# Laying out a collecting tile by branch in a convolution-stem backward kernel

## The chip, the core and the metric

The kernel runs on one core of one Trainium2 chip. The metric is device time in microseconds (us), from the first to the last instruction of one execution; a kernel's time is the median of several executions. The core has four compute engines that work side by side: TensorE (PE) multiplies, VectorE (DVE) and ScalarE (ACT) work element by element and empty the accumulators (PSUM) of PE, GpSimd (POOL) fills and issues transfers. SyncE (SP) computes nothing; its queue issues most DMA transfers. Each engine runs its own list of instructions strictly in order, and an instruction starts when the semaphores that it names have reached their values.

## The reference

The forward pass is a one-dimensional convolution (31 taps, stride 2, 256 channels in and out, 2 sequences of 16000 rows), then a normalisation over time per channel, then GELU. The kernel returns the forward output and the gradients of the input `x`, the weights and the normalisation's scale and shift:

```python
h = jnp.einsum('blc,cd->bld', x[:, 0:s * L:s, :], w[0])
for i in range(1, K):
    h = h + jnp.einsum('blc,cd->bld', x[:, i:i + s * L:s, :], w[i])
...
_out, _vjp = jax.vjp(_f, x, w, gn_gamma, gn_beta)
_grads = _vjp(grad_out)
```

Nearly everything is bfloat16; products are accumulated in float32.

## The kernel before, in words

One big tile named `arena` (211104 bytes on each of the 128 partitions) holds nearly all working data. The function `sb(offset, shape)` cuts views out of it by byte offset, and different stages reuse the same bytes. In the profile, therefore, almost every operand is called `arena`, and work is told apart by its line.

The program is planned first and emitted afterwards. A `Plan` collects all operations; a table of 3528 numbers, `SEQUENCE`, then gives the one order in which they are emitted. So each engine's list is fixed by that table. The semaphore waits are not written in the kernel: the framework adds them when an operation touches bytes of a tile that an earlier operation of another engine or of a DMA reads or writes.

The stages are: forward (matmuls at line 564), input gradient (matmuls at line 1244, stages G0 and G1), weight gradient (line 1522). The change lies in the first part of the input gradient, G0, which runs from about 410 to 605 us and covers three quarters of sequence 0. Interleaved with it, DVE and ACT still work off the GELU backward of sequence 1 (function `gelu_unit`: L922 and L920, L925, L927 and L929, L931, five L935, L946 and L948). The last L935 of each unit needs a piece of `grad_out` that arrives transposed by DMA (L355). Its result is written to a buffer in memory by a DMA of SP (`dyd`).

G0 has six rounds, numbered here 0 to 5: three chunks `c`, two halves `pr` each. The convolution is computed in the manner of a fast (Toom-like) product, with three branches in the order B, A, C, and each branch has leaves A and C beside a shared middle leaf. For branch B the two results are kept in float32 in the tile `GRB` (ACT, L659). For branches A and C, a result that PE has left in PSUM is added to `GRB` by one DVE instruction, L1347, and written to the tile `HO` as bfloat16. A round thus has four such evacuations, written here branch/leaf: A/A, A/C, C/A, C/C; 24 in the six rounds. After both leaves of a branch are there, one SP transfer of 512 KB stores that branch's half rows to `out_1` (L1350 in the source, recorded as L350, the line of the helper `load`). There is one `HO` for all rounds.

The table `SEQUENCE` mixes the rounds' steps. In round 4 the order is A/A, C/A, A/C, store A, C/C, and the store of C comes after A/A of round 5. In round 5 it is A/A, store C of round 4, A/C, C/A, store A, C/C; the store of C comes much later.

Steps that the prediction names: the seed of a branch (`g_seed`, ACT L659 from PSUM to PSUM) copies PSUM banks after the middle leaf and can only write banks that DVE has emptied; the middle leaf's own copy is ACT L1277; `first`, `second`, `third` (L1142, L1192) are DVE differences that make PE's operands; L513 are DVE sums of weights; `dl_turn` transposes planes by SP (L355) and stores them by POOL (`dld`). In the round after the sixth (stage G1) the tile `HO` is replaced by two tiles `HOS[0]` and `HOS[1]` on the same bytes, with the evacuation at L1331.

Of the kernel before, what the change touches and what calls it, by code (L numbers as in the profile page):

```python
# [20 lines left out]
A, B_, C_ = 0, 1, 2  # L21
# [5 lines left out]
def dve(n, rate=2):  # L27
    return 0.155 + n * {1: 0.001035, 2: 0.00052, 4: 0.00029}[rate]
# [161 lines left out]
class Plan:  # L190
# [34 lines left out]
    def add(self, eng, dur, outs, ins, fn, dma=None, slack=None, ns=28.0, tp=112.0):  # L225
        i = len(self.ops)
        preds = set()
        rd = set(c for ap in ins for c in self.cells(ap))
        wr = set(c for ap in outs for c in self.cells(ap))
        for c in rd:  # L230
            preds.update(self.lastw.get(c, ()))
        for c in wr:
            if c[1] != "dram":
                preds.update(self.lastw.get(c, ()))
            preds.update(self.readers.get(c, ()))
        for c in wr:
            if c[1] == "dram" and not self.readers.get(c):
                self.lastw.setdefault(c, []).append(i)
            else:
                self.lastw[c] = [i]  # L240
                self.readers[c] = []
        for c in rd - wr:
            self.readers.setdefault(c, []).append(i)
        preds.discard(i)
        f = sys._getframe(1)
        kind = self.stage + " " + f.f_code.co_name + " " + f.f_back.f_code.co_name
        if eng == "PE":
            self.pe += dur
            self.npe += 1
        self.ops.append(dict(eng=eng, kind=kind, part=self.part, dur=dur, fn=fn, preds=preds, dma=dma, ns=ns, tp=tp, at=self.pe, hold=-1 if eng == "PE" else self.hold,  # L250
                             slack=self.slack if slack is None else slack))
        return i
# [16 lines left out]
def conv_stem_kernel(  # L269
# [16 lines left out]
    P = 128  # L286
# [38 lines left out]
    def sb(off, *shape, dt=BF16):  # L325
        n = int(np.prod(shape)) * (2 if dt == FP32 else 1)
        assert off % 32 == 0 and off + 2 * n <= AR, (off, shape)
        v = arena[:, off // 2:off // 2 + n]
        if dt == FP32:
            v = v.bitcast(FP32)  # L330
        if len(shape) == 1:
            return v
        names = "abcdefg"[:len(shape)]
        return v.rearrange("p (" + " ".join(names) + ") -> p " + " ".join(names), **dict(zip(names, shape)))
# [7 lines left out]
    def load(out, in_, nbytes, run, eng="SP", slack=None, own=False):  # L342
        if plan.stage in ONE and nbytes > 4096 and not own:
            eng = "SP"
        e = {"SP": nc.sync, "POOL": nc.gpsimd, "ACT": nc.scalar}[eng]
        pk = 8192 if run >= 4096 else 4096 if eng == "POOL" else run
        np_ = nbytes / pk
        ns = (PKS if out.space == bass.MemoryType.DRAM else PK)[pk]
        add(eng, {"POOL": 0.74, "SP": 0.46 + 0.00016 * np_, "ACT": 0.4}[eng], [out], [in_],
            lambda: e.dma_start(out=out, in_=in_), dma=np_ * ns / 16e3 * 1.03, ns=ns, tp=SH[pk], slack=slack)  # L350
# [36 lines left out]
    GL = {B_: sb(198656, 2, 2, 2, EM), A: sb(202816, 2, 2, 2, EM), C_: sb(102656, 2, 2, 2, EM)}  # L387
    GU = {B_: sb(206976, 2, 2, EM), A: sb(106816, 2, 2, EM), C_: sb(108928, 2, 2, EM)}
    GRB = sb(111040, 2, 2, 512, dt=FP32)
    HO = [sb(119232, 2, 4, 512)]  # L390
    GREG = 127424
    W2DO = {MIR[br]: sb(o, 2, 2, 512) for br, o in zip(ORDER, (94336, GREG, GREG + 28928))}
    W2DC = {MIR[br]: sb(o, 2, 2, 512) for br, o in zip(ORDER, (98432, GREG + 4096, GREG + 33024))}
# [246 lines left out]
    def flat2(ps):  # L640
        return ps[:].rearrange("p a f -> p (a f)")
# [15 lines left out]
    def keep(out, ps, scale=1.0):  # L657
        add("ACT", act(1024), [out], [ps],
            lambda: nc.scalar.activation(out=out, in_=ps, func=ACT.Copy, scale=scale))  # L659
# [679 lines left out]
    def g_evac(b, c, pr, br, lf, ps):  # L1339
        if br == B_:  # L1340
            keep(GRB[:, 0 if lf == A else 1].rearrange("p e f -> p (e f)"), flat2(ps))
            return
        ho = HO[pr % len(HO)]
        k = (0 if br == A else 1) + (0 if lf == A else 2)
        g = GRB[:, 0 if lf == A else 1]
        add("DVE", dve(1024, 1), [ho[:, :, k, :]], [ps[:], g],
            lambda: nc.vector.tensor_tensor(out=ho[:, :, k, :], in0=ps[:], in1=g, op=ALU.add))  # L1347
        if lf == C_:
            k0 = 0 if br == A else 1
            dst = bass.AP(tensor=out_1.tensor, offset=out_1.offset + (b * T + 4096 * c + 2048 * pr) * C + 512 * k0,  # L1350
                          ap=[[16 * C, P], [1024, 4], [1, 512]])
            load(dst, ho.rearrange("p e (j k) f -> p (e j) (k f)", k=2)[:, :, 512 * k0:512 * k0 + 512], P * 4096, 1024, "SP", slack=60.0)

    def w2_outer(brs):
        for br in brs:
# [12 lines left out]
    def input_grad():  # L1368
# [3 lines left out]
        for c in range(3):  # L1372
            plan.part = c
            first, second, third, planes, leaf = g_sums(c)
            for pr in range(2):
                at, o = run_of(P * pr), P * pr
                for br in ORDER:
                    px, pt = slots4(i)
                    if pr == 0:
                        first(br)  # L1380
                        third(br)
                    g_three_b(px, br, B_, planes(br, B_), at)
                    if pr == 0:
                        second(br, A)
                    if last:
                        last(A)
                    g_three_ac(px, br, B_, GU[br], at)
                    if pr == 0:
                        second(br, C_)
                    if last:  # L1390
                        last(C_)
                    g_seed(px, pt, False)

                    def last(lf, c=c, pr=pr, br=br, px=px, pt=pt, pl=planes, o=o):
                        ps = pt if lf == A else px
                        g_leaf(ps, br, lf, pl(br, lf), o, False)
                        g_evac(0, c, pr, br, lf, ps)
                    i += 1
                    yield 0, c, pr, br, leaf
# [426 lines left out]
def kernel(tc, x, w, gn_gamma, gn_beta, grad_out,  # L1826
                                                             out_0, out_1, out_2, out_3, out_4):
    return conv_stem_kernel(tc, x, w, gn_gamma, gn_beta, grad_out, out_0, out_1, out_2, out_3, out_4)
# [30 lines left out]
```

## Time and profile before

| what | value |
|---|---|
| median of 3 executions | 1127.28 us (1124.99 to 1130.75) |
| profiled execution, first to last instruction | 1123.8 us |
| PE busy | 1090.1 us (97%) |
| DVE busy | 1029.6 us (92%) |
| ACT busy | 561.9 us (50%) |
| POOL busy | 128.3 us (11%) |
| evacuations L1347 | 24, 1217 ns each (median), from 433.7 to 597.0 us |

The profiled execution is 3.5 us shorter than the median and 1.2 us shorter than the fastest of the three. In the rows of a timeline, the columns are: start in us, length in us, engine, line, operation, output and input, number of merged instructions; in brackets the engine's idle time just before it and what ended that. An instruction's recorded length overlaps its successor's by some 0.08 us on DVE, so the distance of two starts (1.14 us for L1347) is its cost. The engine name SPq stands for SP's queue: the row is the issue of a transfer, not the transfer.

### The profile page before, as it was taken

The numbers are of one execution on the slowest core, as the hardware profiler recorded it, in microseconds if no ns is written. First come the engines' busy times: TensorE is split into PE (matmuls) and PEld (weight loads), VectorE is DVE, ScalarE is ACT, GpSimd is POOL, SyncE is SP. The second block draws the span as 40 slices with busy tenths as digits, with TensorE's granted clock in tenths as the row PEclk, the third lists the DMA queues.
The fourth block names the chain that finished last, engine by engine and source line by source line (L and its number), as shares of the span: only waits on it lengthen the run. The fifth ranks groups of instructions, "written<-read, shape, count | busy, mean of one in ns | idle before, by whom it ended". The sixth has DMA issues, their size and how long they took to land. (4 is left out here: it accounts for less than half of the span.)

```text
span 1123.8 us, 19279 instructions
## 1 busy us (share of the span) xinstructions
PE 1090.1 (97%) x7670; PEld 755.2 (67%) x7716; DVE 1029.6 (92%) x1028; ACT 561.9 (50%) x836; POOL 128.3 (11%) x212
## 2 busy tenths in 40 slices
PE   6999999999999999999988999999999999999998
PEld 4888899978777884444433444444478886666787
DVE  6997878869999999899988999898999999889998
ACT  2344354477878859777866666574412212112200
POOL 0000000000000012232322233232210000000000
PEclk9999999999999999999999999999999999999999
DMA  9759779776969999999974887989999517999575
GB/s 234 134 154 185 224 174 257 216 169 146 205 171 228 257 355 275 270 251 264 247 205 138 203 203 200 228 200 234 261 325 235 206 53 252 343 315 332 176 224 145
DMA packets 364023, 249.88 MB, mean 222 GB/s; under 512 B 235287, under 2 KB 332829, under 8 KB 362013
## 3 DMA queue, kind: packets, MB, share of 16 engines
q1 hardware_dynamic: 356829, 229.76, 77.2%
q0 software_dynamic: 7104, 18.89, 5.9%
q8 instruction: 60, 0.98, 0.4%
q14 instruction: 30, 0.25, 0.1%
HBM read 109.38 MB, written 83.40 MB: 172 GB/s over the span
## 5 line engine op out<-in xcount | busy, mean ns | idle before, releaser
L564 PE MATMUL ps<-arena 128*128 128x256 bf16 (+4 forms) x3488 | 402.4, 279 | 15.1 <-DMA arena<-in_x_dram 4.7
L1244 PE MATMUL ps<-arena 128*128 128x512 bf16 (+1 forms) x1775 | 388.6, 377 | 10.3 <-ACT ps L659 4.5
L564 PEld LDWEIGHTS <-arena 128*128 128x128 bf16 x3488 | 341.6, 99 | 75.6 <-issue 11.0
L1244 PEld LDWEIGHTS <-arena 128*128 128x128 bf16 x1812 | 177.7, 98 | 220.7 <-issue 13.6
L1522 PE MATMUL ps<-arena 128*128 128x256 bf16 (+1 forms) x2407 | 299.6, 286 | 4.4 <-DVE arena L1592 2.5
L1522 PEld LDWEIGHTS <-arena 128*128 128x128 bf16 x2416 | 235.9, 98 | 68.1 <-DVE arena L1592 3.5
L659 ACT ACTIVATE arena<-ps 128x1024 f32<-128x1024 f32 x126 | 126.7, 1023 | 257.8 <-PE ps L1522 100.6
L525 DVE TENSOR_TENSOR arena<-arena 128x2064 bf16<-128x2064 bf16 (+7 forms) x127 | 158.3, 1273 | 13.4 <-PE ps L564 13.0
L350 POOL DMA_DIRECT2D dld<-arena x144 | 104.6, 728 | 253.6 <-DMA arena<-arena 205.7
L935 DVE TENSOR_TENSOR arena<-arena 128x2048 bf16<-128x2048 bf16 (+1 forms) x80 | 95.1, 1194 | 2.6 <-ACT arena L927 1.1
L1474 DVE TENSOR_TENSOR arena<-arena 128x4096 bf16<-128x4096 bf16 (+1 forms) x50 | 87.6, 1772 | 5.8 <-DMA arena<-in_x_dram 5.7
L1321 DVE TENSOR_TENSOR ps<-ps,arena 128x1024 f32<-128x1024 f32 x60 | 72.5, 1225 | 7.4 <-PE ps L1244 5.3
L1192 DVE TENSOR_TENSOR arena<-arena 128x1032 bf16<-128x1032 bf16 (+1 forms) x110 | 72.2, 688 | 2.0 <-PE ps L1244 1.8
L679 ACT ACTIVATE arena<-ps 128x512 bf16<-128x512 f32 (+1 forms) x64 | 37.1, 582 | 52.0 <-PE ps L564 48.9
L359 POOL MEMSET arena<- 128x128 bf16 (+9 forms) x31 | 8.6, 298 | 410.8 <-DVE arena L525 257.4
L1624 ACT COPY ps<-ps 128x256 f32<-128x256 f32 x54 | 19.1, 359 | 71.8 <-PE ps L1522 70.7
L1331 DVE TENSOR_TENSOR arena<-ps,arena 128x1024 bf16<-128x1024 f32 x40 | 48.3, 1216 | 6.0 <-PE ps L1244 5.7
L1608 DVE TENSOR_TENSOR arena<-arena 128x2048 bf16<-128x2048 bf16 x42 | 50.5, 1215 | 0.0
L634 ACT ACTIVATE arena<-ps 128x512 f32<-128x512 f32 x64 | 33.8, 599 | 26.9 <-PE ps L564 16.9
L600 ACT ACTIVATE ps<-ps 128x256 f32<-128x256 f32 x72 | 26.6, 370 | 40.3 <-PE ps L564 39.2
L1592 DVE TENSOR_TENSOR arena<-arena 128x2048 bf16<-128x2048 bf16 x38 | 45.5, 1216 | 0.2
L925 DVE SCALAR_TENSOR_TENSOR arena<-arena 128x2048 bf16<-128x2048 bf16 (+1 forms) x16 | 35.8, 2235 | 10.6 <-ACT arena L922 10.4
(89 smaller groups left out, 792.2 us busy)
## 6 DMA issues: line engine op xcount, KB each, us to landing
arena<-in_x_dram SPq DMA_DIRECT2D x82, 512.0 KB
dld<-arena POOLq DMA_DIRECT2D x144, 128.0 KB, 4.0
out_dram<-arena SPq DMA_DIRECT2D x31, 512.0 KB
arena<-hd SPq DMA_DIRECT2D x24, 512.0 KB
arena<-dld SPq DMA_DIRECT2D x18, 640.0 KB
arena<-dld SPq DMA_DIRECT2D x18, 576.0 KB
hd<-arena SPq DMA_DIRECT2D x8, 1024.0 KB
dyd<-arena SPq DMA_DIRECT2D x16, 512.0 KB
```

Of the source, the lines that this page charges most:

```text
L350: lambda: e.dma_start(out=out, in_=in_), dma=np_ * ns / 16e3 * 1.03, ns=ns, tp=SH[pk], slack=slack)
L525: lambda: nc.vector.tensor_tensor(out=o, in0=a, in1=b, op=ALU.add))
L564: yield nc.tensor.matmul(ps[:, dh, cs], lhsT=wt, rhs=mv, start=s0, stop=False, skip_group_check=True)
L659: lambda: nc.scalar.activation(out=out, in_=ps, func=ACT.Copy, scale=scale))
L935: add("DVE", dve(nf), [o], [a, b_], lambda: V.tensor_tensor(out=o, in0=a, in1=b_, op=op))
L1192: lambda: nc.vector.tensor_tensor(out=o, in0=a, in1=b, op=ALU.subtract))
L1244: yield nc.tensor.matmul(ps[:, e, 0:wide], lhsT=lt, rhs=mv, start=s0, stop=False, skip_group_check=True)
L1321: lambda ps=ps, g=g: nc.vector.tensor_tensor(out=ps[:], in0=px[:], in1=g, op=ALU.add))
L1331: lambda: nc.vector.tensor_tensor(out=ho[:, :, k, :], in0=ps[:], in1=g, op=ALU.add))
L1474: add("DVE", dve(o.free_size()), [o], [a, b], lambda: nc.vector.tensor_tensor(out=o, in0=a, in1=b, op=ALU.add))
L1522: yield nc.tensor.matmul(ps[:, s, c0:c1], lhsT=lt, rhs=mv, start=s0, stop=False, skip_group_check=True)
L1608: add("DVE", dve(2048), [o], [u, v], lambda o=o, u=u, v=v: nc.vector.tensor_tensor(out=o, in0=u, in1=v, op=ALU.subtract))
```

## The change

The tile `HO` has 4096 bfloat16 per partition. Before, its axes are (row half `e`, slot of 4, 512), and the slot is branch + 2 x leaf: for each `e`, the four results A/A, C/A, A/C, C/C lie behind one another, so the two branches interleave. In the change, the axes are (branch, `e`, leaf, 512): the first 4096 bytes belong to branch A, the next 4096 to branch C. The evacuation writes two runs of 512 as before, now 1024 elements apart and not 2048. The store reads the branch's 2048 elements, which before were four runs of 512 with gaps and now lie behind one another. The destination of the store is unchanged.

```diff
-    HO = [sb(119232, 2, 4, 512)]
+    HO = [sb(119232, 2, 2, 2, 512)]
...
-        ho = HO[pr % len(HO)]
-        k = (0 if br == A else 1) + (0 if lf == A else 2)
-        g = GRB[:, 0 if lf == A else 1]
+        ho = HO[pr % len(HO)][:, 0 if br == A else 1]
+        k = 0 if lf == A else 1
+        g = GRB[:, k]
         add("DVE", dve(1024, 1), [ho[:, :, k, :]], [ps[:], g],
             lambda: nc.vector.tensor_tensor(out=ho[:, :, k, :], in0=ps[:], in1=g, op=ALU.add))
         if lf == C_:
             k0 = 0 if br == A else 1
             dst = bass.AP(tensor=out_1.tensor, offset=out_1.offset + (b * T + 4096 * c + 2048 * pr) * C + 512 * k0,
                           ap=[[16 * C, P], [1024, 4], [1, 512]])
-            load(dst, ho.rearrange("p e (j k) f -> p (e j) (k f)", k=2)[:, :, 512 * k0:512 * k0 + 512], P * 4096, 1024, "SP", slack=60.0)
+            load(dst, ho.rearrange("p e k f -> p (e k) f"), P * 4096, 1024, "SP", slack=60.0)
```

No instruction is added, removed or moved on any engine; the waits differ. Below, rows with - are the program before, rows with + the changed one. A name DMAHWn is the semaphore of one of eight counters that SP's transfers take in turn; a transfer's own row lists its counter first. PE and Activation are those engines' semaphores, DVE likewise.

On DVE, at the last evacuation (C/C) of round 4:

```order
 L935 TENSOR_TENSOR arena<-arena 128x8x232 [waits DMAHW3_49,Activation_49]
 L931 TENSOR_SCALAR arena<-arena 128x8x232
-L1347 TENSOR_TENSOR arena<-ps,arena 128x2x512 [waits DMAHW6_49,PE_49]
+L1347 TENSOR_TENSOR arena<-ps,arena 128x2x512 [waits PE_49]
 L935 TENSOR_TENSOR arena<-arena 128x8x232 [waits DVE_49,Activation_49]
```

The wait on counter 6, which round 4's store of branch A takes, is no longer there; the place in the order is the same.

On DVE, at C/A and C/C of round 5 (the two L1347; the L935 between them stands in both programs):

```order
 L935 TENSOR_TENSOR arena<-arena 128x8x232 [waits DVE_49]
+L1347 TENSOR_TENSOR arena<-ps,arena 128x2x512 [waits DMAHW6_49,PE_49]
+L935 TENSOR_TENSOR arena<-arena 128x8x232 [waits DMAHW1_49,DMAHW0_49,DMAHW3_49,DVE_49,Pool_49]
 L1347 TENSOR_TENSOR arena<-ps,arena 128x2x512 [waits PE_49]
-L935 TENSOR_TENSOR arena<-arena 128x8x232 [waits DMAHW1_49,DMAHW0_49,DMAHW3_49,DVE_49,Pool_49]
-L1347 TENSOR_TENSOR arena<-ps,arena 128x2x512 [waits DMAHW7_49,PE_49]
 L948 ISA arena,esum_122<-arena 128x4x232 [waits DMAHW4_49,DVE_49]
```

Before, C/C waits on counter 7, which round 5's store of branch A takes; now it waits for PE alone, and C/A names counter 6, which round 4's store of branch C takes.

On SP, the store of branch C of round 4 and the store of branch A of round 5, each with a neighbour:

```order
-L350 DMA out_dram<-arena 512x1x512 [waits DMAHW6_49,DVE_49]
+L350 DMA out_dram<-arena 512x1x512 [waits DMAHW6_49]
 L355 DMA_TRANSPOSE arena<-arena 128x4x128 [waits DMAHW7_49]
...
-L350 DMA out_dram<-arena 512x1x512 [waits DMAHW7_49,DVE_49]
+L350 DMA out_dram<-arena 512x1x512 [waits DMAHW7_49]
 L355 DMA_TRANSPOSE arena<-arena 128x4x128 [waits DMAHW0_49]
```

The wait on DVE stands before both stores in the program before and at neither in the changed one.

## The prediction

> **What bounds the kernel now.** I read the waits of DVE and SP first, to see whether the tile's stores hold anything up at all. The columns are: who waited for what, total us, times, longest.
>
> ```profile
> DVE arena L1347 <- DMA out_dram<-arena: 6.6, 3, 3.7
> SPq L350 <- DVE arena L1347: 3.4, 3, 1.8
> ```
>
> So three of the 24 evacuations wait for a store to land, 6.6 us in all, and three times SP's queue is held until an evacuation is done. Next the engines' timelines, to place them. DVE:
>
> ```profile
> 553.92 2.36 DVE L1347 TENSOR_TENSOR arena<-ps,arena 128x1024 bf16<-128x1024 f32 x2 [0.18 <-DMA out_dram<-arena]
> 563.34 0.64 DVE L931 TENSOR_SCALAR arena<-arena 128x1856 bf16<-128x1856 bf16 x1
> 567.72 1.22 DVE L1347 TENSOR_TENSOR arena<-ps,arena 128x1024 bf16<-128x1024 f32 x1 [3.74 <-DMA out_dram<-arena]
> 568.86 4.65 DVE L935 TENSOR_TENSOR arena<-arena 128x1856 bf16<-128x1856 bf16 x4
> 590.85 1.11 DVE L935 TENSOR_TENSOR arena<-arena 128x1856 bf16<-128x1856 bf16 x1
> 592.11 1.22 DVE L1347 TENSOR_TENSOR arena<-ps,arena 128x1024 bf16<-128x1024 f32 x1
> 593.25 1.11 DVE L935 TENSOR_TENSOR arena<-arena 128x1856 bf16<-128x1856 bf16 x1
> 597.02 1.22 DVE L1347 TENSOR_TENSOR arena<-ps,arena 128x1024 bf16<-128x1024 f32 x1 [2.66 <-DMA out_dram<-arena]
> ```
>
> The long waits are C/C of round 4 (567.72) and C/C of round 5 (597.02). Both wait for the store of branch A of their own round, issued just before. C/C writes none of the bytes that this store reads; in the old layout the two sets only interleave. Between these two rows DVE has no idle time except 0.15 us at 592.11 (590.85 + 1.11 = 591.96). Is DVE what PE waits for? PE's own rows:
>
> ```profile
> 555.62 13.11 PE L1244 MATMUL ps<-arena 128*128 128x512 bf16 x58
> 570.10 9.23 PE L1244 MATMUL ps<-arena 128*128 128x256 bf16 x44 [1.36 <-ACT ps L659]
> 580.31 2.75 PE L1244 MATMUL ps<-arena 128*128 128x512 bf16 x11 [0.99 <-ACT ps L1277]
> 585.04 10.26 PE L1244 MATMUL ps<-arena 128*128 128x512 bf16 x39 [1.98 <-ACT ps L659]
> 595.77 4.48 PE L1244 MATMUL ps<-arena 128*128 128x512 bf16 x20 [0.46 <-ACT arena L659]
> 601.39 0.59 PE L1244 MATMUL ps<-arena 128*128 128x512 bf16 x2 [1.15 <-ACT ps L659]
> 603.26 6.65 PE L1244 MATMUL ps<-arena 128*128 128x512 bf16 x29 [1.28 <-DVE arena L1192]
> 610.35 29.91 PE L1244 MATMUL ps<-arena 128*128 128x512 bf16 x136 [0.45 <-ACT arena L659]
> ```
>
> PE stands still 7.67 us in seven pieces, all between 568.7 and 610.4, mostly for ACT. ACT in turn:
>
> ```profile
> 569.04 1.01 ACT L659 ACTIVATE ps<-ps 128x1024 f32<-128x1024 f32 x1 [4.20 <-DVE arena L1347]
> 573.54 0.98 ACT L946 ACTIVATE arena<-arena 128x928 bf16<-128x928 bf16 x1 [2.56 <-DVE arena L935]
> 579.69 0.57 ACT L1277 COPY ps<-ps 128x512 f32<-128x512 f32 x1
> 582.33 1.75 ACT L927 ACTIVATE arena<-arena 128x1856 bf16<-128x1856 bf16 x1 [1.11 <-DVE arena L925]
> 583.98 1.01 ACT L659 ACTIVATE ps<-ps 128x1024 f32<-128x1024 f32 x1
> 599.40 1.02 ACT L659 ACTIVATE arena<-ps 128x1024 f32<-128x1024 f32 x1 [1.28 <-DVE esum L948]
> 600.32 1.02 ACT L659 ACTIVATE ps<-arena 128x1024 f32<-128x1024 f32 x1
> ```
>
> Each of ACT's waits here ends with a DVE instruction. The chain is: store lands, DVE evacuates, ACT seeds, PE goes on; DVE carries it from 567.7 to 603. Outside this stretch the evacuations cost PE nothing, as the windows show (columns: stretch, its length, busy us and instructions of PE, weight loads, DVE, ACT, POOL, granted clock, DMA share, GB/s):
>
> ```profile
> 530.00:550.00 20.00, 19.89 (x94) 9.23 (x95) 19.00 (x22) 16.22 (x18) 5.41 (x9) 1.00 0.98 243
> 560.00:570.00 10.00, 8.69 (x40) 3.86 (x40) 5.55 (x6) 5.29 (x5) 0.87 (x2) 1.00 1.07 247
> 584.00:586.00 2.00, 0.96 (x4) 0.44 (x4) 2.00 (x5) 2.00 (x3) 1.79 (x3) 0.89 1.18 241
> 586.00:588.00 2.00, 2.00 (x7) 0.68 (x5) 2.00 (x4) 1.14 (x2) 0.10 (x1) 0.50 0.80 231
> 588.00:590.00 2.00, 2.00 (x9) 0.81 (x8) 2.00 (x3) 0.00 (x0) 0.00 (x0) 0.76 0.33 66
> 600.00:610.00 10.00, 7.43 (x33) 3.04 (x32) 9.89 (x22) 6.42 (x8) 1.54 (x3) 1.00 0.27 87
> ```
>
> PE is full from 530 to 550. In the three short windows the clock falls to half and costs 2 x (0.11 + 0.50 + 0.24) = 1.7 us of PE's work.
>
> **The change part by part.** *Cost of the instructions: none.* The new write pattern, two runs 1024 elements apart, is the one that L1331 has already:
>
> ```profile
> L1347 DVE TENSOR_TENSOR arena<-ps,arena x24: 1207/1217/1225, 433.7 to 597.0; 128x1024 bf16<-128x1024 f32 x24
> L1331 DVE TENSOR_TENSOR arena<-ps,arena 128x1024 bf16<-128x1024 f32 x40 | 48.3, 1216 | 6.0 <-PE ps L1244 5.7
> ```
>
> 1217 against 1216 ns, 24 times 1 ns at most. The store moves the same runs of 512 elements to the same addresses.
>
> *Round 4, C/C.* Without the store's wait it is ready when L931 ends, 563.34 + 0.64 = 563.98: 3.74 us earlier. Could PE hold it instead? Between the matmuls that it needs and 568.73 (555.62 + 13.11) PE issues 40 more; at 13.11 / 58 = 0.226 us those take 9.0 us, so they were done at 559.7. No. It ends at 565.1 (spacing 1.14), the seed of 569.04 runs at 565.2 to 566.3, and PE, which needs it at 568.73, has it: the 1.36 us of idle time go.
>
> *Carried on.* DVE's run from 568.86 starts 3.74 us earlier. ACT's L946 waits only for it and follows; so L1277 moves from 579.69 to about 576, while PE, now at 568.73 + 9.23 = 577.96, no longer waits: 0.99 us gone. PE ends the next 2.75 us at 580.7. The seed of 583.98 hangs on DVE's L925 through L927, so it comes 3.74 us earlier, ends at 581.25, and PE idles some 0.6 us and not 1.98. The pause of 2.75 + 0.6 us before the half-clock stretch is then shorter than the gaps of 1.15 and 1.28 us with 0.59 us of work between them at 601 to 603, where the last window shows clock 1.00. I take the clock as staying full.
>
> *Round 5, C/A and C/C.* C/A needs 24 matmuls from 581.3: at 0.226 us until 586.7, while DVE comes at 591.96 - 3.74 = 588.2. So DVE also gains the 0.15 us. The L935 after it follows and ends at 590.5. C/C's store wait of 2.66 us goes; PE's eight further matmuls are done at 588.5. So C/C starts at 590.5, not 597.02: 6.5 us earlier.
>
> *Up to 603.* The L1192 that PE waits for at 603.26 stands in DVE's list behind C/C with no idle time of DVE before it. Its one neighbour that could hold it is the seed on DVE behind ACT's 599.40: ACT waits there for DVE's L948, which is 6.5 us earlier, and PE reaches the banks at about 592. PE starts at 596.8, not 603.26.
>
> *SP.* The stores were also held by false reads:
>
> ```profile
> 578.58 0.56 SPq L350 DMA_DIRECT2D out_dram<-arena  x1
> ...
> 580.70 2.63 SPq L355 DMA_TRANSPOSE arena<-in_grad_out_dram  x2
> 583.38 8.11 SPq L355 DMA_TRANSPOSE arena<-arena  x5
> 593.36 0.55 SPq L350 DMA_DIRECT2D out_dram<-arena  x1
> ```
>
> 593.36 is the end of C/A (592.11 + 1.22 = 593.33), which this store of branch A doesn't read. Freed, it leaves when the transposes ahead of it are issued, 1.8 us earlier by the wait row and 3.7 more with DVE. What is queued behind it, a transpose for `dld` and the `dyd` and `yd` stores, goes earlier too. Nothing on PE's path waits for it first; DMA is idle enough (0.27 from 600 to 610). I count 0.
>
> *The other waits.* The 0.18 us at 553.92 lie under full PE until 568.73: 0. The waits that move to C/A of the next round name stores that landed long before (round 4's C store, issued at 578.58, against 588.2): 0, and 3.7 us if one lasted as long as the longest.
>
> *Does it reach the end?* From 603 PE has one pause of 0.45 us in 37 us, SP's queue and DMA have just run dry, so all that follows starts from the same state, earlier. The chain of waits goes on in compute and in transfers that compute releases:
>
> ```profile
> 642.52 10.74 PE ps L1244 x49
> 804.31 6.26 DMA out_dram<-arena
> ```
>
> Sum: 3.74 + 2.66 = **6.4 us** (0.15 more at best, as much kept for small waits). Checked on PE: of 7.67 us of idle time about 2.5 stay (0.6, some 0.35 after C/A, 1.1 before 596.8, 0.45), so 5.2, and 1.7 of clock: 6.9. The lower holds, since DVE is last at 603. Bounds: 1.36 (only the first pause goes) and 7.67 + 1.7 = 9.4. The profiled 1123.8 would become 1117.4; against the median of 1127.28 it is 1120.9, 0.57% less.
>
> [...] Both drops in this trace followed a pause of 2 us: 1.98 at 585.04, and
>
> ```profile
> 394.28 5.89 PE L564 MATMUL ps<-arena 128*128 128x231 bf16 x41 [2.02 <-ACT ps L600]
> ```
>
> [...]
>
> **The rivals.** (a) *The clock still drops* in the burst from 581.3. C/A then has its banks at 588.4 and C/C at 590.2, so DVE is as before; but PE comes 1.7 us later to the banks behind ACT's 599.40 copy, and DVE's seed waits about 1.0 us. Gain 5.4, 1121.9.
>
> (b) *Another wait ends last.* The L935 at 568.86 and 593.25 need `grad_out` transposes, and the L1192 before 603 overwrite what a `dyd` store reads. If the second gain is lost so, 3.7 remain: 1123.6; if both, 1.4: 1125.9. For: DMA is full (1.07) from 560 to 570. Against: SP issues these earlier too.
>
> (c) *Nothing moves:* the framework still treats the branches as overlapping, or PE's later work absorbs it: 1127.3. Against: the wait on counter 6 is gone from C/C's row.
>
> (d) *Slower:* the freed stores and the transposes between them meet in the stretch from 570 to 590, and each lands later, the `grad_out` ones among them. In full DMA the store before 567.72 held DVE 3.74 us, in lighter traffic the one issued at 593.36 held it 2.66: about 1.1 us per transfer. The two stores and the seven transposes of the SP rows, one behind another, would cost 9 x 1.1 = 9.9, less the 6.4 gained: 1130.8. Slower beyond 0.5% it becomes from (5.6 + 6.4) / 9 = 1.33 us each; at 1.5 it ends at 1134.4. Against: in the trace before, DVE reached both L935 without waiting for a transpose.
>
> **How the numbers follow.** Forecast 0.55, (a) 0.14, (b) 0.17, (c) 0.09, (d) 0.05. About 0.5% (5.6 us, a time below 1121.6) is what a measurement of this kernel can tell from no change. The forecast lies 0.7 us beyond that line, so of its 0.55 I count 0.45 as faster and 0.10 as no change; (a), at the line, gives 0.07 to each; (b) and (c) are no change. Faster 0.52, no change 0.43, slower 0.05. The range: the upper bound of the gain gives 1127.28 - 9.4 = 1117.9, and 0.9 for the spread of runs makes 1117.0; upward it takes in both times of (b) and ends at 1126.5, which leaves out most of (c) and (d).
>
> **What would show it.** Right: no store among what L1347 waits for; C/C of round 4 within 0.1 us of the L931 before it; round 5's C/C some 6.5 us earlier; PE idle from 568 to 610 near 2.5 us; clock 1.00 throughout; store A of round 5 issued before C/A ends. Wrong: L935, L1192 or L1321 there waiting for a DMA or ACT by more than 1 us, or later PE pauses that add up to what was gained.

## The result and the profile after

| | before | after |
|---|---|---|
| median of 7 executions each, same chip | 1127.28 us (1124.45 to 1130.75) | 1119.80 us (1118.07 to 1122.41) |
| ratio | | 0.9929, 95% interval 0.9915 to 0.9944 |
| profiled execution, span | 1123.8 us | 1118.2 us |
| DVE's waits for a store, L1347 | 6.6 us | none |
| PE idle from 568.7 to 610.4 us | 7.67 us | 1.89 us |

The medians are 7.5 us apart (0.66%). The ratio, which is not that of the two medians, puts the gain at 0.71% (8.0 us), with an interval from 0.56% to 0.85%. A span is 1.8 us shorter than the time of the same execution (1118.2 and 1120.03 us for the profiled one of the change). The profile before, with its span of 1123.8 us, is therefore of an execution of about 1125.6 us: that is 1.7 us below the median, and not below the fastest of the three, as "Time and profile before" has it, where a span was compared with times.

The waits of the changed kernel, of DVE's instructions first, then of SP's queue (who waited for what, total us, times, longest):

```profile
DVE arena L1347 <- ACT arena L946: 1.0, 1, 1.0
DVE arena L1331 <- DMA out_dram<-arena: 0.5, 2, 0.3
DVE arena L935 <- ACT arena L929: 0.4, 1, 0.4
...
SPq L350 <- DVE arena L1347: 0.6, 1, 0.6
```

No store is left among what L1347 waits for. Its one wait, for ACT, stood in the kernel before too (1.1 us). SP still waits for an evacuation once, 0.6 us instead of 3.4. New is the 0.36 us at L935, and the next rows show where it lies. DVE's timeline after:

```profile
562.90 0.64 DVE L931 TENSOR_SCALAR arena<-arena 128x1856 bf16<-128x1856 bf16 x1
563.46 1.22 DVE L1347 TENSOR_TENSOR arena<-ps,arena 128x1024 bf16<-128x1024 f32 x1
565.03 4.66 DVE L935 TENSOR_TENSOR arena<-arena 128x1856 bf16<-128x1856 bf16 x4 [0.36 <-ACT arena L929]
...
587.85 1.22 DVE L1347 TENSOR_TENSOR arena<-ps,arena 128x1024 bf16<-128x1024 f32 x1
588.99 1.12 DVE L935 TENSOR_TENSOR arena<-arena 128x1856 bf16<-128x1856 bf16 x1
590.02 1.22 DVE L1347 TENSOR_TENSOR arena<-ps,arena 128x1024 bf16<-128x1024 f32 x1
595.51 1.30 DVE L1192 TENSOR_TENSOR arena<-arena 128x1032 bf16<-128x1032 bf16 x2
```

C/C of round 4 starts right behind L931, 4.26 us earlier than before (567.72 - 563.46): 3.74 us are the wait that is gone, the other 0.5 us lie ahead of L931 and come up again below. C/A of round 5 is 4.26 us earlier too, and C/C of round 5 is 7.00 us earlier (597.02 - 590.02). The L1192 for which PE waits at the end of the stretch follows without a gap, 7.01 us earlier (602.52 - 595.51). PE and SP after:

```profile
549.83 31.03 PE L1244 MATMUL ps<-arena 128*128 128x512 bf16 x145
581.22 13.95 PE L1244 MATMUL ps<-arena 128*128 128x512 bf16 x62 [0.36 <-ACT ps L659]
596.26 6.65 PE L1244 MATMUL ps<-arena 128*128 128x512 bf16 x30 [1.09 <-DVE arena L1192]
603.35 8.95 PE L1244 MATMUL ps<-arena 128*128 128x512 bf16 x41 [0.44 <-ACT arena L659]
```

```profile
576.11 0.59 SPq L350 DMA_DIRECT2D out_dram<-arena  x1
587.56 0.60 SPq L350 DMA_DIRECT2D out_dram<-arena  x1
590.13 0.52 SPq L350 DMA_DIRECT2D dyd<-arena  x1
```

Three short pauses of PE are left of seven. Store A of round 5 leaves at 587.56, before C/A ends (587.85 + 1.22), and the `dyd` store behind it at 590.13. The clock, in the columns of the prediction's windows:

```profile
560.00:570.00 10.00, 10.00 (x49) 4.67 (x48) 8.80 (x10) 6.62 (x6) 0.79 (x2) 1.00 1.11 238
580.00:590.00 10.00, 9.64 (x45) 4.19 (x43) 10.00 (x13) 4.13 (x5) 3.69 (x6) 1.00 0.95 207
600.00:610.00 10.00, 9.56 (x45) 4.17 (x44) 9.83 (x23) 9.54 (x11) 1.74 (x3) 1.00 0.35 82
```

PE and DVE are both nearly full now, at full clock. So 7.0 us are gained by 603. The two spans differ by 5.6 us only: this one profile gave some 1.5 us back between 805 and 842, at the start of the weight gradient. PE there, after and before:

```profile
811.51 1.03 PE L1522 MATMUL ps<-arena 128*128 128x256 bf16 x8 [2.10 <-DMA arena<-dld]
```

```profile
816.80 1.03 PE L1522 MATMUL ps<-arena 128*128 128x256 bf16 x8 [0.41 <-DMA arena<-dld]
```

A transfer of planes is waited for 2.10 us instead of 0.41. Two later profiles of the changed kernel, below, have no such wait.

### The profile page after: what moved, and what is told of

It reads as the page before. It is cut to its first block, busy times and chain, and to the rows that moved or that the text cites. A ratio compares the mean times of both kernels' runs of the same rounds, so it can differ in the third digit from the quotient of the medians.

```text
span 1118.2 us, 19323 instructions
## 1 busy us (share of the span) xinstructions
PE 1088.8 (97%) x7716; PEld 753.4 (67%) x7716; DVE 1029.7 (92%) x1028; ACT 562.5 (50%) x836; POOL 129.7 (12%) x212
## 5 line engine op out<-in xcount | busy, mean ns | idle before, releaser
L935 DVE TENSOR_TENSOR arena<-arena 128x2048 bf16<-128x2048 bf16 (+1 forms) x80 | 95.2, 1196 | 2.9 <-ACT arena L927 1.0
L1192 DVE TENSOR_TENSOR arena<-arena 128x1032 bf16<-128x1032 bf16 (+1 forms) x110 | 72.5, 691 | 2.0 <-PE ps L1244 1.8
L1331 DVE TENSOR_TENSOR arena<-ps,arena 128x1024 bf16<-128x1024 f32 x40 | 48.4, 1219 | 6.0 <-PE ps L1244 5.4
L1608 DVE TENSOR_TENSOR arena<-arena 128x2048 bf16<-128x2048 bf16 x42 | 50.5, 1217 | 0.3 <-DMA out_dram<-arena 0.3
L1592 DVE TENSOR_TENSOR arena<-arena 128x2048 bf16<-128x2048 bf16 x38 | 45.6, 1219 | 0.2
L925 DVE SCALAR_TENSOR_TENSOR arena<-arena 128x2048 bf16<-128x2048 bf16 (+1 forms) x16 | 35.8, 2237 | 10.2 <-ACT arena L922 9.9
```

Of the source, the lines that this page charges most:

```text
L935: add("DVE", dve(nf), [o], [a, b_], lambda: V.tensor_tensor(out=o, in0=a, in1=b_, op=op))
L1192: lambda: nc.vector.tensor_tensor(out=o, in0=a, in1=b, op=ALU.subtract))
L1608: add("DVE", dve(2048), [o], [u, v], lambda o=o, u=u, v=v: nc.vector.tensor_tensor(out=o, in0=u, in1=v, op=ALU.subtract))
```

## The experiments

Four questions were open: which rounds carry the gain; whether it is DVE's waits or SP's freed queue; whether one wait undone costs what it was; and why the medians differ by more than the two profiles. The ratios are to the kernel before on the same chip, whose median was 1128.09 us for the first four, and 1129.06 us for the four after them.

### Which rounds carry it

In the first kernel, rounds 4 and 5 keep the old layout; in the second, rounds 0 to 4 do. The condition is the only difference of the two: the second has `if (c, pr) == (2, 1):` where the first has `if c < 2:`. Against the kernel before (`...` stands for lines left out; `sep` is the tile with the axes of the new layout, `src` what the store reads):

```diff
-        k = (0 if br == A else 1) + (0 if lf == A else 2)
...
+        if c < 2:
+            k = 0 if lf == A else 1
...
+            o, src = sep[:, :, k, :], sep.rearrange("p e k f -> p (e k) f")
+        else:
+            k = (0 if br == A else 1) + (0 if lf == A else 2)
...
+            o = ho[:, :, k, :]
...
```

> The new layout in rounds 0 to 3, the old one in rounds 4 and 5. Theory: PE is full there, so at most the 0.9 us by which DVE was ahead at L925 (558 us) before the first long wait: 1126 to 1128. Rival (the gapless store or the freed SP queue helps in each round): 1122 to 1125.

> The old layout in rounds 0 to 4, the new one in round 5 alone. Theory: round 4's wait of 3.7 us stays, round 5's of 2.7 goes: 1124 to 1125.5, with the clock's drop to half still there. Rival (one wait only moves the loss to the other): 1126.5 to 1128.

Rounds 0 to 3 alone: 1127.95 us, ratio 1.0002 (0.9989 to 1.0015), no change. Round 5 alone: 1123.60 us, ratio 0.9956 (0.9938 to 0.9973), which is 4.5 us between the medians: more than the wait of 2.66 us, and 0.4 us below the range expected. DVE's waits for a store in the two:

```profile
DVE arena L1355 <- DMA out_dram<-arena: 5.2, 2, 2.7
```

```profile
DVE arena L1355 <- DMA out_dram<-arena: 4.5, 1, 4.5
```

Both long waits are still there in the first and one, round 4's, in the second. The gain lies in the last two rounds, as the prediction had it: where DVE waits for no store, these runs show nothing that the layout itself is worth, within 1.7 us either way.

### DVE's waits or SP's queue

Two factors changed at once: DVE no longer waits for store A, and SP no longer waits for A/A and C/A. Each was undone alone, by sending evacuations to the slots that they had in the old layout, so that the wait is a true one. In the first kernel, C/C of rounds 4 and 5 writes such slots, in the second A/A and C/A of round 5; the rows of `out_1` concerned are not the reference's. The second also leaves out the line that asserts that the table keeps the plan's order, so its line numbers are one lower. Against the change:

```diff
+        o = ho[:, :, k, :]
+        if c == 2 and (br, lf) == (C_, C_):
+            o = HO[0].rearrange("p r e k f -> p (r e k) f").rearrange("p (e k) f -> p e k f", e=2)[:, :, 3, :]
...
```

```diff
+        o = ho[:, :, k, :]
+        if (c, pr) == (2, 1) and lf == A:
+            o = HO[0].rearrange("p r e k f -> p (r e k) f").rearrange("p (e k) f -> p e k f", e=2)[:, :, 0 if br == A else 1, :]
...
```

> The changed layout, but C/C of rounds 4 and 5 writes its results into slots 3 and 7 of the tile, so that half of them lie in branch A's part and the instruction truly waits for the store of branch A; the rows of C/C in out_1 for these two rounds are therefore not the reference's. SP's stores stay free of the reads of A/A and C/A. Theory (the two waits of DVE are the whole gain): within 1.5 us of the kernel before, 1126 to 1128; DVE waits again about 3.5 and 2.7 us for a store; the granted clock falls to half after the pauses. Rival (the gain comes from the freed SP queue or from the store's gapless source): 1119 to 1122, as the changed kernel.

> The change, but A/A of round 5 writes old slots 0 and 4 and C/A old slots 1 and 5 (the rows of out_1 of round 5 are not the reference's): store C of round 4 now truly has to wait for A/A of round 5 and store A of round 5 for C/A, as the old layout did falsely, while C/C waits for no store. So DVE's waits are gone and SP's queue is held. Theory (a held queue sends the dyd store late, and L1192 before 603 waits for it): DVE is 6 to 7 us early up to about 597 and gives about 2 us back at L1192, so the time is about 2 us above the change, 1121.5 to 1124. Rival (the prediction's step: SP's freeing is worth nothing): as the change, 1119 to 1121.5.

> The change once more, as the level for the other three runs on the same chip. Theory: 1119 to 1121.5, and a ratio near the first one's 0.9929; the granted clock of this profile may show a half-rate stretch that the first did not, since the same 2.0 us pause of PE was followed by one in two of six traces. Rival (the clock's drop at 585 is gone for good, as the prediction had it): full clock from 380 to 620 in this profile too.

| | DVE waits | DVE free |
|---|---|---|
| SP held | 1 (before) | 0.9921 (0.9908 to 0.9934), 1120.33 us |
| SP free | 0.9959 (0.9943 to 0.9975), 1123.83 us | 0.9911 (0.9897 to 0.9924), 1119.26 us |

The right column is from one chip, the lower left corner from another, each against the kernel before on its own chip. The repeat of the change (lower right) came out as expected, its half-rate stretch included (granted clock 0.57 from 394 to 398 us).

With DVE free and SP held, nearly the whole gain is there; the difference to the change is 1.1 us, and the two intervals overlap. Store A of round 5 is truly held: it leaves at 590.08, when C/A ends (588.84 + 1.21 = 590.05). What remains of it in the trace:

```profile
590.08 0.55 SPq L349 DMA_DIRECT2D out_dram<-arena  x1
590.68 1.51 SPq L354 DMA_TRANSPOSE arena<-arena  x1
592.29 0.54 SPq L349 DMA_DIRECT2D dyd<-arena  x1
...
596.90 1.30 DVE L1191 TENSOR_TENSOR arena<-arena 128x1032 bf16<-128x1032 bf16 x2 [0.31 <-DMA dyd<-arena]
```

The held store sends the `dyd` store 2.2 us later than in the change's first profile (592.29 against 590.13), and L1192 waits 0.31 us for it. I had expected 2 us there; the rival, which was the prediction's step "I count 0", came out.

The other corner is the surprise. With SP free and DVE's waits kept, 4.6 us are gained by the ratio (4.3 between the medians), where the theory had said 2 at most and its rival 6 or more. DVE and SP in that kernel:

```profile
566.52 1.23 DVE L1350 TENSOR_TENSOR arena<-ps,arena 128x1024 bf16<-128x1024 f32 x1 [3.25 <-DMA out_dram<-arena]
593.50 1.23 DVE L1350 TENSOR_TENSOR arena<-ps,arena 128x1024 bf16<-128x1024 f32 x1 [0.79 <-DMA out_dram<-arena]
```

```profile
590.12 0.59 SPq L350 DMA_DIRECT2D out_dram<-arena  x1
```

The store of round 5 no longer waits for C/A (it is issued at 590.12, while C/A runs from 590.47), lands earlier, and so the wait that was kept shrinks from 2.66 to 0.79 us. Freeing DVE and freeing SP are thus two ways to the same 1.9 us in round 5, and they don't add. Store waits of 3.25 + 0.79 = 4.04 us are left, against 6.4 in the first profile of the kernel before and 7.0 in the mean of its four, which come below. The clock explains none of the rest. PE is slowed in this kernel too: its 30 matmuls from 599.75 us take 8.34 us where the change takes 6.65, and the mean clock of the profile is 0.997. The 1.69 us are about what the half-rate stretches in the first profile of the kernel before would cost (3.41 us each, so 1.7 us of PE's work, by estimate). DVE then waits for PE:

```profile
606.40 0.70 DVE L1192 TENSOR_TENSOR arena<-arena 128x1028 bf16<-128x1028 bf16 x1 [1.53 <-PE ps L1244]
```

The profiles thus account for some 3.2 us: 3.0 of store waits, 0.8 of a wait for ACT that comes below, less 0.6 for the wait for PE. The interval of the 4.6 us reaches from 2.8 to 6.4, so whether the rest is more than noise stays open.

### The stores moved behind C/C, in the old layout

Here the layout stays as before, and the table moves store A behind C/C in both rounds (1867 and 1944 are the stores, 1884 and 1971 the C/C). C/C then doesn't wait for a store, but the stores wait for C/C.

```diff
-    ... 1880, 1867, 1928, 1919, 1886, 1501, 1929, 1499, 1925, 1500, 1920, 1884, 1511,
+    ... 1880, 1928, 1919, 1886, 1501, 1929, 1499, 1925, 1500, 1920, 1884, 1867, 1511,
...
-    ... 1968, 1944, 1964, 2021, 1965, 1528, 2028, 1973, 1971, 2018, ...
+    ... 1968, 1964, 2021, 1965, 1528, 2028, 1973, 1971, 1944, 2018, ...
```

> The old interleaved layout; in the table of the order, the store of branch A in rounds 4 and 5 is put behind C/C of the same round, so C/C has no store before it to wait for. Theory: the gain of the changed kernel without its layout, 1119 to 1122; C/C of round 4 within 0.5 us of the DVE work before it. Rival (freed SP queue or gapless source): 1126 to 1129, since SP now waits for C/C too.

1124.17 us, ratio 0.9967 (0.9955 to 0.9979): less than half of the gain, and in neither of the two ranges expected. SP, DVE and PE:

```profile
593.78 0.55 SPq L350 DMA_DIRECT2D out_dram<-arena  x1
594.38 0.63 SPq L350 DMA_DIRECT2D dyd<-arena  x1
```

```profile
592.54 1.21 DVE L1347 TENSOR_TENSOR arena<-ps,arena 128x1024 bf16<-128x1024 f32 x1
600.38 1.31 DVE L1192 TENSOR_TENSOR arena<-arena 128x1032 bf16<-128x1032 bf16 x2 [2.26 <-DMA dyd<-arena]
```

```profile
601.14 8.34 PE L1244 MATMUL ps<-arena 128*128 128x512 bf16 x30 [3.46 <-DVE arena L1192]
```

The wait moved instead of going: store A waits for C/C's end, the `dyd` store stands behind it in SP's queue and leaves at 594.38, 4.3 us later than in the change, and L1192, which overwrites what `dyd` reads, waits 2.26 us. That is the wait of the prediction's rival (b), at its second place. The wait ends 6.0 us after the issue here and 4.6 us after it in the kernel with SP held (596.90 - 592.29); in the change's first profile L1192 comes 5.4 us after the issue (595.51 - 590.13) and doesn't wait. By the shorter of these times the change has 0.8 us to spare at this place, by the longer none. The clock adds to it, by the same estimate: PE's 30 matmuls take 8.34 us here too, where the change takes 6.65, and a later L1192 waits 1.53 us for PE.

### One wait kept at a time

Against the change; the second kernel has `(2, 1)` where the first has `(2, 0)`:

```diff
+        o = ho[:, :, k, :]
+        if (c, pr) == (2, 0) and (br, lf) == (C_, C_):
+            o = HO[0].rearrange("p r e k f -> p (r e k) f").rearrange("p (e k) f -> p e k f", e=2)[:, :, 3, :]
...
```

> The change, but C/C of round 4 alone writes old slots 3 and 7, which store A of its round reads, so it truly waits for that store; the rows of out_1 of that evacuation are not the reference's. The two stores on SP's queue are free. Theory (DVE's two waits are the gain, SP's freeing adds a little on round 5): round 4's wait comes back at 3 to 4 us, round 5's does not, so the time is 3 to 4 us above the change, 1123 to 1124.5. Rival (the gain is SP's freeing, DVE's waits only shift it): as the change, 1119 to 1121.

> The same for C/C of round 5 alone (rows of out_1 of that evacuation are not the reference's). Theory: freed SP issues store A of round 5 at about 587.5, before C/A ends; in the change's trace DVE reaches C/C at 590.0 and the store lands 2.7 to 3.7 us after its issue, so the wait that comes back is 0.2 to 1.3 us and not 2.66: the time is 0.2 to 1.3 us above the change, 1120 to 1122. Rival (the prediction's sum, in which SP's freeing counts nothing): 2.66 us above the change, 1122.5 or more.

Round 4's wait kept: 1122.14 us, ratio 0.9940 (0.9923 to 0.9956). Round 5's kept: 1122.01 us, ratio 0.9937 (0.9920 to 0.9954). They are 2.9 and 2.8 us above the change on that chip, 5.7 together; with both kept, on another chip, the ratio is 0.0048 above the change's, or 5.4 us. DVE of the first, then DVE and PE of the second:

```profile
567.98 1.23 DVE L1350 TENSOR_TENSOR arena<-ps,arena 128x1024 bf16<-128x1024 f32 x1 [4.57 <-DMA out_dram<-arena]
```

```profile
591.59 1.23 DVE L1350 TENSOR_TENSOR arena<-ps,arena 128x1024 bf16<-128x1024 f32 x1 [1.39 <-DMA out_dram<-arena]
604.41 0.70 DVE L1192 TENSOR_TENSOR arena<-arena 128x1028 bf16<-128x1028 bf16 x1 [1.46 <-PE ps L1244]
...
597.83 8.27 PE L1244 MATMUL ps<-arena 128*128 128x512 bf16 x29 [1.28 <-DVE arena L1192]
```

Round 4's wait has its cost, 2.9 us, just below the 3 to 4 expected. Round 5's wait is 1.39 us, near the expected 0.2 to 1.3, but the time is 2.8 us up, as the rival said, though not for its reason. The PE row shows the other half: the same 29 or 30 matmuls take 8.27 us where the change takes 6.65, behind PE's pauses of 1.13 and 1.28 us, which I put down to the clock again (its mean over the profile is 0.998), and DVE then waits 1.46 us for PE. 1.39 + 1.46 = 2.85. The medians alone would not decide it: the six executions of this kernel reach from 1118.92 to 1125.38 us, and its interval overlaps the change's.

### Where the clock falls

So the clock was not done with after all. The kernel before was profiled three times more, the change once more on the same chip.

> The kernel before once more, for its profile. The change's median gain so far (7.5 and 9.8 us) is more than the 5.5 us by which the two first profiles differ. Theory: the kernel before has more half-rate stretches of the clock (mean clock 0.996 over its runs, against 0.9985 for the change; one stretch of 3.41 us at half rate lowers the mean over 1125 us by 0.0015, so 2.6 stretches against 1.0), and the first profile of it, with two, was a good one: profiles of it show two to four, beside the pauses of PE from 568 to 605 and at 394, and the span grows by 0.7 to 1.7 us with each. Rival: no more than one stretch each, and what grows is a wait for a transfer.

> As the run before it: the second of three profiles of the kernel before. Theory: two to four half-rate stretches, most of them from 568 to 610. Rival: one or none.

> As the two runs before it: the third of three profiles of the kernel before. Theory: two to four half-rate stretches, most of them from 568 to 610. Rival: one or none.

> The change once more, for its third profile on the same chip as the three of the kernel before. Theory: at most one half-rate stretch ahead of the end, at 394 or at about 596, and none from 568 to 590, where PE no longer stands still; DVE's C/C of round 5 some 7 us before that of the kernel before. Rival: as many stretches as the kernel before.

The times were 1128.71, 1125.12 and 1128.41 us for the kernel before, and 1118.26 us for the change, each of one execution. The stretch from 550 to 612 us in the first profile of the kernel before and in these three, in this order (the eighth column is the granted clock):

```profile
550.00:612.00 62.00, 54.13 (x238) 24.04 (x242) 53.22 (x72) 39.39 (x46) 16.81 (x26) 0.97 0.73 194
```

```profile
550.00:612.00 62.00, 53.59 (x235) 23.31 (x234) 50.94 (x64) 36.67 (x44) 16.86 (x26) 0.94 0.74 195
```

```profile
550.00:612.00 62.00, 54.71 (x244) 24.12 (x243) 53.34 (x73) 39.26 (x46) 16.76 (x26) 0.97 0.73 194
```

```profile
550.00:612.00 62.00, 52.01 (x231) 22.75 (x229) 51.07 (x64) 36.50 (x44) 16.81 (x26) 0.97 0.75 195
```

And in the three profiles of the change (the first, the repeat beside the kernel with SP held, the last):

```profile
550.00:612.00 62.00, 60.00 (x278) 27.01 (x277) 60.29 (x83) 46.37 (x53) 19.64 (x30) 1.00 0.82 209
```

```profile
550.00:612.00 62.00, 58.99 (x270) 26.73 (x274) 60.48 (x84) 46.13 (x54) 19.65 (x30) 1.00 0.82 212
```

```profile
550.00:612.00 62.00, 60.01 (x278) 27.03 (x277) 60.29 (x83) 45.98 (x54) 19.64 (x30) 1.00 0.81 208
```

In all four profiles of the kernel before the clock falls somewhere in this stretch, in none of the three of the change. In the two short executions (spans of 1123.8 and 1123.3 us) it falls between 580 and 590, where it is 0.83 in the mean, in the first of them at 585.56; in the two long ones (1126.9 and 1126.6) it falls behind 600, at about 602 and 605. The place decides what it costs. Before 590, PE's lost time lies under DVE's chain, which then waits 2.66 us for the store anyway. Behind 600, DVE has no wait left to hide it, and waits for PE itself, as DVE's row in the first of the two long ones shows; the matching row of the first profile (at 608.41) has no wait:

```profile
611.65 0.70 DVE L1192 TENSOR_TENSOR arena<-arena 128x1028 bf16<-128x1028 bf16 x1 [2.01 <-PE ps L1244]
```

In the second long one it is 1.53 us. The expectation of two to four half-rate stretches was too high: the three new profiles have one each ahead of the end, between 568 and 610 as it said, of which one lasts some 6.8 us (clock 0.71 from 600 to 605 and 0.61 from 605 to 610), twice the others (0.83 from 580 to 590; 0.66 from 605 to 610). The change's last profile has one at 394 (0.58 from 394 to 398) and none from 568 to 590, as expected. The store waits also vary; the rows of the three new profiles:

```profile
DVE arena L1347 <- DMA out_dram<-arena: 7.4, 2, 3.9
```

```profile
DVE arena L1347 <- DMA out_dram<-arena: 6.5, 2, 3.9
```

```profile
DVE arena L1347 <- DMA out_dram<-arena: 7.5, 2, 4.3
```

With the 6.4 of the first profile the mean is 7.0 us; the wait for a slowed PE (2.01 and 1.53 in two of four) adds 0.9. A third term lies ahead of round 4's C/C, where L925 waits for ACT's L922. The row of the first profile of the kernel before:

```profile
558.39 2.09 DVE L925 SCALAR_TENSOR_TENSOR arena<-arena 128x1856 bf16<-128x1856 bf16 x1 [0.97 <-ACT arena L922]
```

In its other three profiles the wait is 0.67, 0.72 and 0.84 us, in the three of the change 0, 0.38 and 0: that is 0.7 us less in the mean. It is 0.56 us or more in all seven profiles with the old layout in round 4, and 0.42 or less in all seven with the new one. It goes with the layout, then, but no run shows what shortens it. The new wait at L935 (0.36, 0 and 0.35) takes 0.2 us back.

Together the terms make 8.4 us. The L1192 that can wait for PE starts at 608.41, 611.65, 608.69 and 611.82 in the kernel before and at 601.41, 601.95 and 601.81 in the change, 8.4 us earlier in the mean. The mean spans, 1125.15 us for four profiles and 1117.1 for three, differ by 8.05, since the first profile of the change gives its 1.5 us back later. These profiles are from more than one chip. The medians differ by 7.5 us on the first chip and by 9.8 on that of the repeat (0.9911). Why that chip shows more stays open: the mean clock of the timed executions there was 0.996 for the kernel before and 0.9985 for the change, lower for the kernel before than in its profiles (0.997 to 0.998), but no trace shows where those stretches fell.

## Why the prediction was right, and where it was off

**Forecast.** 1120.9 us was predicted and 1119.80 measured; the forecast was the likeliest case, and its mechanism, DVE's two waits for a store, is what the runs show. That the number came so near is partly luck: the sum took its sizes from one profile and left out three smaller terms, which add up to 1.4 us.

**Cost of the instructions: right.** L1347 takes 1219 ns against 1217, and rounds 0 to 3 alone change nothing (1.0002).

**Round 4: right.** C/C was to start at 563.98 when L931 ends, and starts at 563.46 behind it, since L931 itself comes 0.5 us earlier: L925's wait for ACT, 0.97 us before, is gone, which the prediction did not foresee. A small wait took a place that the prediction had not seen: the next L935 waits 0.36 us for ACT's L929, since DVE came earlier and ACT not quite as much. Round 5's C/A at 588.2 (587.85), C/C at 590.5 (590.02), PE at 596.8 (596.26): all within 0.6 us. PE's idle time was to be near 2.5 us and is 1.89.

**The sum: right in kind, too small in size.** The term 3.74 + 2.66 = 6.4 took the store waits of one execution for the kernel's. Four profiles show 6.4 to 7.5, mean 7.0, and the one at hand was the lowest. Two terms are missing, both gains: 0.9 us in the mean for DVE's wait for a slowed PE and 0.7 us for L925's wait for ACT. Less the 0.2 us of L935's new wait, that makes 8.4 us by 610, in the means of four profiles and three.

**The clock: right in place, wrong in worth and in reason.** "I take the clock as staying full" held in this stretch in three of three profiles. But the prediction counted the clock on PE's side alone, as 1.7 us at 585, where it was hidden under DVE's wait. What it misses is that the half-rate stretch of the kernel before also falls at 602 to 605, where it costs 1.5 to 2.0 us: a further gain of 0.9 us in the mean. And its reason, the length of the pause, is not enough: the pause of 2.02 us at 392 was in the trace of before followed by a drop, and in the first of the change not. No run shows what decides it. From 550 to 612 PE's longest pause is 1.09 us in the first profile of the change and 1.08 us in the last, and the clock stays at 1.00 in all three; whether luck had a part in that stays open. PE's row of the change, and the window there in the change and before:

```profile
394.79 3.33 PE L564 MATMUL ps<-arena 128*128 128x231 bf16 x32 [2.02 <-ACT ps L600]
```

```profile
394.00:398.00 4.00, 3.21 (x32) 3.08 (x32) 4.00 (x3) 2.73 (x7) 0.45 (x1) 1.00 1.03 410
```

```profile
394.00:398.00 4.00, 3.72 (x21) 2.96 (x21) 3.97 (x5) 2.25 (x5) 0.45 (x1) 0.57 1.03 394
```

**SP: "I count 0" right, for the change as a whole.** Holding SP's stores again costs 0.3 us in the trace and 1.1 us in the medians, which the intervals can't tell from none. It is not nothing by itself: with DVE's waits kept, the same freedom is worth 1.9 us of round 5's wait.

**It reaches the end: right,** except for the 1.5 us that the first profile of the change gave back at the weight gradient's start and the two later ones did not.

**The rivals.** (a), the clock still dropping in the burst from 581.3, happened in none of the change's three profiles (clock 1.00 from 580 to 590), and no run shows what a drop there would cost. Behind 597.83, in the kernel with round 5's wait kept, PE's slower matmuls cost DVE a wait of 1.46 us; the prediction gave 1.0 for its own place. (b) did not happen at either place, but moving the stores shows its second place: 2.26 us at L1192. (c) and (d) fell: no freed transfer met another to DVE's cost.

## What to carry to other kernels

A wait row that names a transfer which the waiting instruction doesn't need is worth a look at the layout: two results that interleave in one tile can be held against each other, though they share no byte, and here laying them out apart bought 0.7% with no instruction added, removed or moved. Ask of each such wait who is late next (here PE, through ACT), and undo it alone before adding gains up, since two freed waits may lead to the same time. One profile gives the size of a wait for one execution only; before a per cent is split into terms, take two or three. The same holds for the clock: here PE's pause of 2.0 us at 392 was followed by a half-rate stretch in three profiles and by full clock in two.

## What the runs showed of the hardware

In the first profile of the kernel before, the half-rate stretches ahead of the end reach from 394.42 to 397.83 us and from 585.56 to 588.98, 3.4 us each. In the two others whose clock falls behind 600 us, the shares of the windows add up to 3.4 us (0.66 from 605 to 610) and 6.8 us (0.71 and 0.61 from 600 to 610).

Where they lie differs from execution to execution, and the length of the pause alone doesn't tell. PE's pause at 392 was 2.02 us in the first profile of the kernel before and in all three of the change, and 2.03 in the first repeat of the kernel before. The clock from 394 to 398 was then 0.57 in the first, 1.00, 0.57 and 0.58 in the three of the change, and 1.00 in the repeat. The first profile of the kernel before has pauses of 0.99 and 1.98 us ahead of 585, and its clock falls there; it has pauses of 1.15 and 1.28 us ahead of 603, and its clock is 1.00 from 600 to 610. The two long ones have 3.16 and 3.12 us at the latter place, and there the clock falls. In the change, the pauses from 550 to 612 are 0.36, 1.09 and 0.44 us in the first profile and 0.35, 1.08 and 0.44 in the last, and its clock stays at 1.00. What decides between a drop and none, no run shows.

A queue that is held delays what stands behind it: the `dyd` store left at 590.1 us in the change, at 592.3 with SP held and at 594.4 with the stores moved, and L1192 then waited 0, 0.31 and 2.26 us.
